# Landmark attention into a Fourier-mixed MLP: eight second halves of each weight matrix made on another engine, and the pseudo-inverse's product split off

## The chip, the core and the metric

The kernel runs on one core of a Trainium2 chip. The core has five engines that run side by side and signal each other by semaphores: TensorE (PE, matmuls; PEld is its loading of weights), VectorE (DVE), ScalarE (ACT), GpSimd (POOL) and SyncE (SP), which here issues the DMAs. Matmuls write to PSUM, eight banks of 128 partitions by 512 f32; all else lies in SBUF. The metric is device time in microseconds of one execution; the span that the profile shows runs from the first to the last instruction of it.

## The reference

There are two parts. The first is Nyström attention for 8 batches, 8 heads, 576 tokens of 64 channels, with 32 landmarks, each the mean of 18 tokens:

```python
A  = softmax(q    @ k_lm.T / 8)      # 576 x 32
Bm = softmax(q_lm @ k_lm.T / 8)      # 32 x 32
C  = softmax(q_lm @ k.T / 8)         # 32 x 576
Z  = Bm.T / (norm1(Bm) * norminf(Bm) + 1e-6)
for _ in range(6):
    Z = 2 * Z - Z @ Bm @ Z
x  = A @ Z @ C @ v
```

The second takes the result as rows of 512 (the heads side by side), applies a Fourier transform over tokens and one over channels, and keeps the real part; `u = x + mixed`; the rows of `u` are normalised to `un`; the output is `u + relu(un @ w1) @ w2`, with `w1` of 512 x 2048 and `w2` of 2048 x 512. The weights come as float64.

## The kernel before

**The large matmuls are done in f16, in two halves.** A number is scaled by a power of two, `hi` is its f16 rounding, and `lo` the f16 rounding of the difference; a product is then three f16 products (`mm3`). `split` (line 209) makes the halves: ScalarE writes `hi`, then VectorE writes `lo = src * scale - hi`.

**Weights (thread `weights`, line 233).** Each matrix lies in 16 pieces of 128 x 512. A piece arrives as 64-bit numbers, is decoded into f32 by three VectorE instructions and one of ScalarE (lines 250 and 287 to 289), and lies then in slot `f + 1` of its matrix. When all pieces of a matrix are decoded, their largest magnitude gives the scale (`scale`, line 260, with a transpose and a small product on TensorE in `pow2`). `halve` (line 268) then splits piece `f` into slot `f`, the two f16 halves side by side where a f32 piece lay before; the next piece's halves overwrite the slot that this piece's source was in. First come the 16 decodes of the first matrix; then, for each of the second matrix's 16 decodes, one `halve` of the first; then the second matrix's 16 `halve`s.

**Attention (threads `attention`, `tokens`, `landmarks`).** `tokens` (line 358) forms landmark sums, the scores A, their exponentials and the token side of the transform. `landmarks` (line 503), spawned by it, computes Bm (four heads to a group, two groups), its row-normalised form `nrm` beside the row sums spread over a diagonal, then for each group the product for C with maximum, exponential and sum (`Ces`, line 540), then the sum over columns `psn` with `ones_bd` (line 568), which gives the factor `ci`, then the transpose `BT` of the block matrix `Bbd`, then transposes of C, then C @ v. With E = I - c B B^T and R = c C v, the six steps of the iteration are carried out on R: `RE` holds E's 32 condensed columns beside R's 64, and each step multiplies both by E (line 621): one product of 96 columns for each group, then VectorE masks E into blocks and adds R, and ScalarE copies the condensed E. `Bbd` applied to the result gives W (line 636), its scale, its halves `Wx` and `Wt`, and their products with the transform (`WC`); `mix` forms `u`, and `norm` the statistics of its rows, `un`, and its two halves, which DMA transposes bring to `unT`. For batch 0 `norm` takes the statistics on ScalarE, for the others with BATCH_NORM_STATS2 on VectorE (line 754).

**MLP (thread `mlp`, line 803).** Rows go in 18 chunks of 256. A chunk has eight steps: a step of the first layer uses two pieces of `w1` (24 matmuls of 256 columns into a PSUM bank of `ps_h`, which has two; then ReLU and halves on ScalarE and VectorE), a step of the second (`second`, line 809) two pieces of `w2` (12 matmuls of 512 columns into `acc`). Each step waits until its pieces have been split (`split_w`). The first chunk keeps all eight hidden tiles until the second matrix is there, four of them in `mid` buffers, of which there are seven.

**What sets the order.** The threads are Python generators. A planner (`run`, line 871) keeps a clock `now` and prices for each instruction, and lets the first thread go whose time has come, by priority: `landmarks` before `attention`, `weights` and `mlp`. `till` makes a thread yield until the tiles named are expected to be there. TensorE executes the matmuls in exactly the order in which the planner let them be written; the order of the other engines' instructions is found by the framework's scheduler, with the order of writing as priority. Two waits of the planner hold batch 1 back: in `tokens` (line 414) and in `landmarks` (line 537) it goes on when four steps of the second layer have been written.

Of the kernel before, what the change touches and what calls it, by code (L numbers as in the profile page):

```python
# [10 lines left out]
F32 = mybir.dt.float32  # L11
F16 = mybir.dt.float16
# [113 lines left out]
class Kernel:  # L126
    def __init__(self, ctx, tc, NB, q, k, v, w1, w2, t1, t1t, t2, diag, mask, out):
# [71 lines left out]
    def tr(self, out, a, ident):  # L199
        self.there[out.name] = self.now  # L200
        self.now += 0.11
        self.nc.tensor.transpose(out, a, ident)  # L202
# [30 lines left out]
    def weights(self):  # L233
        nc = self.nc
        V, A = self.V, self.A
        whole = self.whole
        slots = [[t[:, i] for i in range(NF + 1)] for t in whole]
        am = [self.cp.tile([P, NF], F32, name=f"wmax{w}") for w in range(2)]
# [14 lines left out]
        def bound(i):  # L253

            w, f = pieces[i]
            A.activation(mags[i], slots[w][f + 1], AF.Abs, accum_out=am[w][:, f : f + 1])

        es = []

        def scale(w):  # L260
            a2 = self.small(1, "wm2")
            V.tensor_reduce(a2, am[w], AX.X, ALU.max)
            yield self.till(a2)
            e, r = yield from self.pow2(a2, 1, f"wp{w}")
            es.append(e)
            V.tensor_scalar(sc[:, w : w + 1], r[:, 0:1], (2.0**6, 2.0**14)[w], None, ALU.mult)

        def halve():
            w, f = pieces[sum(self.split_w)]
            self.split(hl[w][f][:, 0], hl[w][f][:, 1], slots[w][f + 1], sc[:, w : w + 1])  # L270
            self.split_w[w] = f + 1

        for i, (w, f) in enumerate(pieces):
            while len(mags) < min(2 * NF, i + 1 + PREP):
                j = len(mags)
                while len(self.wraw) < min(2 * NF, j + 1 + AHEAD):
                    self.raw()
                if self.raw_there[j] > self.now:
                    if j > i:
                        break  # L280
# [5 lines left out]
            x, dst = mags[i].bitcast(I32), slots[w][f + 1]  # L286
            V.tensor_scalar(x, x, 3, None, ALU.logical_shift_left)
            V.scalar_tensor_tensor(x, top, -0x80000000, x, ALU.bitwise_and, ALU.bitwise_or)
            V.scalar_tensor_tensor(dst.bitcast(I32), low, 29, x, ALU.logical_shift_right, ALU.bitwise_or)
            if i > 0:  # L290
                bound(i - 1)
            self.decoded = i + 1
            if self.decoded == 2 * NF:
                self.load(1)
            yield max(0.0, max(self.V.free, self.G.free) - self.now - WT)
            if i == NF:
                yield from scale(0)
            if es:
                halve()
                yield max(0.0, max(self.V.free, self.G.free) - self.now - WT)  # L300
# [3 lines left out]
        self.inv2 = sc[:, 2:3]  # L304
        while sum(self.split_w) < 2 * NF:
            halve()
            yield max(0.0, max(self.V.free, self.A.free) - self.now - WT)
# [50 lines left out]
    def tokens(self, b, st):  # L358
# [46 lines left out]
        for g in range(2):  # L405
# [95 lines left out]
        st["tokens"] = [*st["AT"], CS]  # L501

    def landmarks(self, b, st):
# [4 lines left out]
        m4g = lambda m: self.mask4.unsqueeze(1).unsqueeze(3).broadcast_to([P, 2, 4, m])  # L508
        wide = lambda src, m: src.unsqueeze(2).broadcast_to([P, 2, 4, m])
        Bd = sm.tile([P, 2, 32], F32, name="Bd")  # L510
        RE = sm.tile([P, 2, 96], F32, name="RE", bufs=3)
        Ces, crs = [], []
# [23 lines left out]

        while b == 1 and self.seconds < NF // 2 - HB:
            yield 0.5

        for g in range(2):  # L540
# [23 lines left out]
            crs.append(cr)  # L564
        yield self.till(nrm)

        psn = self.psum()
        mm(psn[:, 0:128], self.ones_bd.rearrange("p a b -> p (a b)"), nrm.rearrange("p g x m -> p (g x m)"))
        cm = self.small(4, "cm")
        V.tensor_reduce(cm, psn[:, 0:128].rearrange("p (x m) -> p x m", m=32), AX.X, ALU.max)  # L570
        ci = self.small(2, "ci")
        cmv = cm.rearrange("p (g x) -> p g x", x=2)
        V.tensor_tensor(ci, cmv[:, :, 0], cmv[:, :, 1], ALU.mult)
        V.tensor_scalar(ci, ci, 1e-6, None, ALU.add)
        V.reciprocal(ci, ci)
        nci = self.small(2, "nci")
        V.tensor_scalar(nci, ci, -1.0, None, ALU.mult)
        Bbd = sm.tile([P, 2, 4, 32], F32, name="Bbd", bufs=1)
        V.tensor_tensor(Bbd, wide(nrm[:, :, 0, :], 32), m4g(32), ALU.mult)
        yield self.till(Bbd, Ces[0])  # L580
        pst = self.psum()
        for g in range(2):
            tr(pst[:, 128 * g : 128 * g + 128], Bbd[:, g].rearrange("p a b -> p (a b)"), self.ident)
        BT = sm.tile([P, 2, P], F32, name="BT", bufs=1)
        A.copy(BT.rearrange("p g m -> p (g m)"), pst[:, 0:256])
        ETs = []
        for g in range(2):
# [8 lines left out]
            ETs.append(ET)  # L596
            if g == 0:
                yield self.till(BT, Ces[1])
                pse = self.psum()
                for i in range(2):  # L600
                    mm(pse[:, 128 * i : 128 * i + 128], BT[:, i], BT[:, i])
                E = sm.tile([P, 2, 4, 32], F32, name="E")
                for i in range(2):
                    V.scalar_tensor_tensor(
                        E[:, i].rearrange("p a b -> p (a b)"), pse[:, 128 * i : 128 * i + 128], nci[:, i : i + 1],
                        self.ident, ALU.mult, ALU.add,
                    )
                V.tensor_reduce(RE[:, :, 0:32], E.rearrange("p g a b -> p g b a"), AX.X, ALU.add)
        for g in range(2):
# [3 lines left out]
            for t in range(5):  # L613
                n = P if t < 4 else 64
                for i in range(4):
                    mm(ps[32 * i : 32 * i + 32, 0:64], ETs[g][:n, t, 32 * i : 32 * i + 32], vf[:n, t, 64 * i : 64 * i + 64], t == 0, t == 4)
            V.tensor_scalar(RE[:, g, 32:96], ps[:, 0:64], crs[g], ci[:, g : g + 1], ALU.mult, ALU.mult)
        yield self.till(E, RE)


        for it in range(6):
            c0 = 0 if it < 5 else 32
            ps = self.psum()
            for g in range(2):
                mm(ps[:, 96 * g + c0 : 96 * g + 96], E[:, g].rearrange("p a b -> p (a b)"), RE[:, g, c0:])
            pv = ps[:, 0:192].rearrange("p (g m) -> p g m", g=2)
            nRE = sm.tile([P, 2, 96], F32, name="RE", bufs=3)
            if it < 5:
                E = sm.tile([P, 2, 4, 32], F32, name="E")
                V.tensor_tensor(E, wide(pv[:, :, 0:32], 32), m4g(32), ALU.mult)  # L630
                A.copy(nRE[:, :, 0:32], pv[:, :, 0:32])
            V.tensor_tensor(nRE[:, :, 32:96], RE[:, :, 32:96], pv[:, :, 32:96], ALU.add)
            RE = nRE
            yield self.till(E, RE, more=NM)

        ps, pst = self.psum(), self.psum()
        for g in range(2):
            mm(ps[:, 64 * g : 64 * g + 64], Bbd[:, g].rearrange("p a b -> p (a b)"), RE[:, g, 32:])
# [110 lines left out]
    def norm(self, b, uts):  # L749
# [121 lines left out]
    def run(self):  # L871
# [3 lines left out]
        self.ulive, self.ufree, self.first_done, self.seconds, self.folded = 0, [], 0, 0, -1  # L875
        self.split_w, self.decoded = [0, 0], 0
        self.threads = []
# [83 lines left out]
```

## Time and profile before

| | |
|---|---|
| median of 3 runs | 1067.77 us (1065.95 to 1068.18) |
| the profiled execution | 1067.68 us, span 1065.9 us |
| TensorE, VectorE, ScalarE, GpSimd busy | 981.1, 614.0, 351.7, 126.6 us |
| TensorE's granted clock, mean | 0.960 |
| first matmul of the MLP | 104.70 us |
| first and last `lo` of the first matrix's halves (VectorE) | 92.69, 138.27 us |
| first and last `lo` of the second matrix's halves (VectorE) | 148.31, 187.63 us |
| first matmul of C, batch 1 | 166.81 us |

Times within the profile count from the span's start. A line of the time-ordered view gives start, duration, engine, line of the code (L197 is the helper `mm`, L202 `tr`, L121 the helper that emits for VectorE, ScalarE and GpSimd), operation, written tile `<-` read tiles, shapes, count, and in brackets the idle time before it with what ended it. Since almost all instructions go through helpers, tiles tell the groups apart: `w<-w,wsc` on VectorE is a `lo` of the weights, `h<-unT,w` the first layer, `acc<-w,h` the second, `at<-RE,E` the iteration, `at<-big,qbd` C. A matmul's duration includes its way through the array; how long one holds the engine is read from the start of the next. An f32 product is two MATMUL instructions in the profile.

### The profile page before, as it was taken

Reading aid. Unit: us, or ns where it says so; the run is one execution under the profiler, and the core shown is the slowest. Engines: PE = TensorE matmul, PEld = TensorE weight load, DVE = VectorE, ACT = ScalarE, POOL = GpSimd, SP = SyncE. Lnnn points to the kernel's source line nnn. Section 1 sums busy time; section 2 is a strip of 40 time slices with the busy share of each in tenths; the row PEclk is TensorE's granted clock in tenths of the full one; section 3 lists DMA queues with packets and bytes.
Section 4 is the critical chain, followed back from the end, with each engine's and each line's share of the span. In section 5 each row is a group of like instructions: output and inputs, shape, how many; then the busy total and the mean of one; then the engine's idle time right before and its main releaser. Section 6 shows DMA issues by size and latency. Waiting matters only on the chain.

```text
span 1065.9 us, 19548 instructions
## 1 busy us (share of the span) xinstructions
PE 981.1 (92%) x8008; PEld 681.0 (64%) x8008; DVE 614.0 (58%) x1655; ACT 351.7 (33%) x791; POOL 126.6 (12%) x137
## 2 busy tenths in 40 slices
PE   1553779999999999999999999999999999999998
PEld 0442645677776677766776777667766677766665
DVE  7889888768553476446746574567451654341111
ACT  4566755324221333124322332243312332111110
POOL 0101101021101030110302030104010030110000
PEclk8556989999999999999999999999999999999999
DMA  9824402221401022111502050114111010120000
GB/s 328 311 83 129 141 25 91 70 42 39 152 21 35 26 80 103 21 31 21 179 4 50 11 164 19 40 21 129 64 41 21 21 23 20 21 50 16 5 21 20
DMA packets 85994, 71.70 MB, mean 67 GB/s; under 512 B 56336, under 2 KB 74768, under 8 KB 85776
## 3 DMA queue, kind: packets, MB, share of 16 engines
q1 hardware_dynamic: 85904, 70.45, 22.1%
q8 instruction: 63, 1.03, 0.4%
q14 instruction: 27, 0.22, 0.1%
HBM read 48.02 MB, written 9.44 MB: 54 GB/s over the span
## 4 chain that ended last, share of the span: by engine, by line
PE 86%; DVE 8%; issue 2%; ACT 2%; DMA 1%; POOL 0%; SPq 0%; ACTq 0%; DVEq 0%
PE acc L197 34%; PE h L197 34%; PE at L197 16%; DVE w L121 2%; DVE row L121 2%; DVE mid L121 1%; PE at L202 1%; ACT row L121 1%; DVE lm L121 1%; DMA big<-q_dram 0%; ACT mid L121 0%; DVE asum L121 0%; DVE u L121 0%; DVE RE L121 0%; POOL row L121 0%
## 5 line engine op out<-in xcount | busy, mean ns | idle before, releaser
L197 PE MATMUL h<-unT,w 128*128 128x256 f16 x3456 | 413.5, 274 | 20.3 <-DMA unT<-row 11.5
L197 PEld LDWEIGHTS <-w 128*128 128x128 f16 x3456 | 336.2, 98 | 92.8 <-issue 19.5
L197 PE MATMUL acc<-w,h 128*128 128x512 f16 x1680 | 394.8, 379 | 0.0
L197 PEld LDWEIGHTS <-h 128*128 128x128 f16 x1680 | 161.9, 98 | 160.5 <-issue 3.4
L121 DVE SCALAR_TENSOR_TENSOR h<-h 128x512 f16<-128x512 f32 x140 | 96.5, 689 | 247.5 <-ACT h L121 247.0
L121 ACT ACTIVATE h<-h 128x512 f16<-128x512 f32 x140 | 83.4, 596 | 367.9 <-PE h L197 367.5
L121 POOL TENSOR_TENSOR r<-ve,mhalf 128x2 f32<-128x2 f32 (+1 forms) x20 | 13.7, 683 | 446.7 <-DVE ve L121 446.7
L121 POOL TENSOR_TENSOR row<-row 128x512 f16<-128x512 f32 (+1 forms) x44 | 47.3, 1089 | 44.0 <-ACT row L121 44.0
L197 PEld LDWEIGHTS <-mid 128*128 128x128 f16 x432 | 40.2, 103 | 17.7 <-issue 9.0
L197 PEld LDWEIGHTS <-big 128*128 128x128 f16 (+1 forms) x768 | 41.3, 106 | 13.6 <-issue 2.4
L121 POOL TENSOR_TENSOR mid<-mid,asum 128x512 f32<-128x512 f32 x14 | 15.1, 1080 | 272.2 <-issue 134.5
L121 DVE TENSOR_REDUCE lm<-big 128x32 f32<-128x576 f32 (+1 forms) x48 | 44.2, 945 | 3.3 <-DMA big<-k_dram 3.2
L121 DVE SCALAR_TENSOR_TENSOR row<-at,scw,row 128x262 f32<-128x262 f32 (+1 forms) x48 | 21.4, 486 | 41.4 <-ACT row L121 27.2
L121 ACT CAST row<-row 128x512 f16<-128x512 f32 (+1 forms) x44 | 23.2, 557 | 64.5 <-DVE row L121 63.9
L121 ACT ACTIVATE row<-w 128x512 f32<-128x512 f32 x54 | 33.8, 641 | 22.8 <-DVE w L121 12.4
L197 PE MATMUL at<-RE,E 128*128 128x96 f32 (+1 forms) x192 | 31.1, 288 | 9.0 <-DVE RE L121 9.0
L121 DVE SCALAR_TENSOR_TENSOR u<-at,scw,row 128x128 f32<-128x128 f32 (+3 forms) x120 | 38.9, 389 | 0.0
L121 POOL TENSOR_TENSOR mid<-mid 128x256 f32<-128x256 f32 (+1 forms) x32 | 31.5, 987 | 61.5 <-DVE mid L121 54.0
L197 PEld LDWEIGHTS at<-RE,E 128*128 128x128 f32 x192 | 28.6, 205 | 15.3 <-issue 6.2
L121 DVE TENSOR_TENSOR mid<-mid 128x256 f32<-128x256 f32 x48 | 34.5, 743 | 1.6 <-POOL mid L121 1.4
L197 PE MATMUL at<-mid,big 128*128 128x262 f16 (+1 forms) x288 | 34.3, 293 | 0.0
L121 DVE SCALAR_TENSOR_TENSOR u<-acc,wsc,u 128x512 f32<-128x512 f32 x36 | 26.7, 745 | 11.5 <-PE acc L197 11.3
(167 smaller groups left out, 955.6 us busy)
## 6 DMA issues: line engine op xcount, KB each, us to landing
w<-w_dram SPq DMA_DIRECT2D x22, 512.0 KB, 8.9
big<-v_dram SPq DMA_DIRECT2D x16, 640.0 KB, 9.2
big<-q_dram SPq DMA_DIRECT2D x16, 584.0 KB, 5.2
big<-k_dram SPq DMA_DIRECT2D x16, 576.0 KB, 4.2
out_dram<-u SPq DMA_DIRECT2D x36, 256.0 KB, 2.0
big<-w_dram SPq DMA_DIRECT2D x10, 512.0 KB, 8.2
unT<-row SPq DMA_TRANSPOSE x72, 2.4
t<-t_dram SPq DMA_DIRECT2D x1, 1048.0 KB, 9.2
```

The source lines that it names most:

```text
L121: return call(out, *args, **kw)
L197: self.nc.tensor.matmul(out, a, b, start=start, stop=stop, skip_group_check=True)
L202: self.nc.tensor.transpose(out, a, ident)
```

## The change

1. **Lower halves.** Pieces with odd `f` of both matrices no longer have their `lo` made by VectorE. TensorE multiplies the f32 source by an f32 identity times the scale, adds the f16 product of `hi` with minus the identity into the same PSUM tile (from `ps_h`), and ScalarE copies that tile to `lo`. The first matrix gets one more slot, so its source lies two slots ahead of its halves (`f + 2`) and not one; the second keeps one. In the first matrix an odd piece's TensorE part is written with the next piece's `halve`, in the second at once, behind a `till(hi)`.
2. **The iteration in a thread of its own.** `inverse`, spawned by `landmarks`, carries out the six steps on the condensed P (32 columns) and not on R (64): `EP` of 64 columns holds E and P. The first step multiplies 32 columns, the last 32, those between 64. A block product G = P^T Bbd follows, and `landmarks`, which keeps R apart, waits for G and applies it where it applied `Bbd` before.
3. **Order in `landmarks`.** The sum over columns `psn` and `ci` now come before the products of C.
4. **The second batch.** Both waits of batch 1 end after one step of the second layer, not four.
5. **Statistics.** `norm` uses ScalarE's passes for batch 1 as well as for batch 0.

```diff
-        self.whole = [self.cp.tile([P, NF + 1, 512], F32, name=f"w{w}") for w in range(2)]
+        self.whole = [self.cp.tile([P, NF + 2 - w, 512], F32, name=f"w{w}") for w in range(2)]
...
+        self.minus = self.cp.tile([P, P], F16, name="minus")
+        nc.vector.tensor_scalar(self.minus, self.ident, -1.0, None, ALU.mult)
...
             V.tensor_scalar(sc[:, w : w + 1], r[:, 0:1], (2.0**6, 2.0**14)[w], None, ALU.mult)
+            V.tensor_scalar(scaled[w], self.ident, sc[:, w : w + 1], None, ALU.mult)
...
         def halve():
-            w, f = pieces[sum(self.split_w)]
-            self.split(hl[w][f][:, 0], hl[w][f][:, 1], slots[w][f + 1], sc[:, w : w + 1])
-            self.split_w[w] = f + 1
+            w = 0 if self.begun[0] < NF else 1
+            f = self.begun[w]
+            hi, lo, src = hl[w][f][:, 0], hl[w][f][:, 1], slots[w][f + 2 - w]
+            if f % 2 == 0:
+                self.split(hi, lo, src, sc[:, w : w + 1])
+            else:
+                A.activation(hi, src, AF.Copy, scale=sc[:, w : w + 1])
+            self.begun[w] += 1
+            left.append((w, f, hi, lo, src))
+            while left and (left[0][1] % 2 == 0 or len(left) > 1 - left[0][0] or self.begun[0] == NF):
+                w, f, hi, lo, src = left.pop(0)
+                if f % 2:
+                    yield self.till(hi)
+                    ps = self.ps_h.tile([P, 512], F32, name="h")
+                    self.mm(ps, scaled[w], src, True, False)
+                    self.mm(ps, self.minus, hi, False, True)
+                    A.copy(lo, ps)
+                self.split_w[w] = f + 1
...
-        while b == 1 and self.seconds < NF // 2 - HB:
+        while b == 1 and self.seconds < 1:
             yield 0.5
...
+    def inverse(self, st, nrm, nci):
...
+        for it in range(6):
+            yield self.till(E, EP, banks=1, more=NM)
+            c0, c1 = (0 if it < 5 else 32), (64 if it > 0 else 32)
+            ps = self.psum()
+            for g in range(2):
+                mm(ps[:, 64 * g + c0 : 64 * g + c1], flat(E, g), EP[:, g, c0:c1])
...
+        yield self.till(Pbd, banks=1)
+        ps = self.psum()
+        for g in range(2):
+            mm(ps[:, 128 * g : 128 * g + 128], flat(Pbd, g), flat(Bbd, g))
+        G = sm.tile([P, 2, 4, 32], F32, name="G", bufs=1)
+        A.copy(G.rearrange("p g a b -> p (g a b)"), ps[:, 0:256])
+        st["G"] = G
...
+        self.spawn(self.inverse(st, nrm, nci))
+
+        while b == 1 and self.seconds < 1:
             yield 0.5
...
-            V.tensor_scalar(RE[:, g, 32:96], ps[:, 0:64], crs[g], ci[:, g : g + 1], ALU.mult, ALU.mult)
-        yield self.till(E, RE)
-
-
-        for it in range(6):
-            c0 = 0 if it < 5 else 32
-            ps = self.psum()
-            for g in range(2):
-                mm(ps[:, 96 * g + c0 : 96 * g + 96], E[:, g].rearrange("p a b -> p (a b)"), RE[:, g, c0:])
...
+            V.tensor_scalar(R[:, g], ps[:, 0:64], crs[g], ci[:, g : g + 1], ALU.mult, ALU.mult)
+
+        while "G" not in st:
+            yield 0.3
+        Gt = st["G"]
+        yield self.till(Gt, R, banks=2)
...
-                mm(pst[64 * o : 64 * o + 64, 64 * g : 64 * g + 64].rearrange("p (r m) -> p r m", r=2), RE[:, g, 32:], Bbd[:, g, o::2])
+                mm(pst[64 * o : 64 * o + 64, 64 * g : 64 * g + 64].rearrange("p (r m) -> p r m", r=2), R[:, g], Gt[:, g, o::2])
...
-        if b == 0:
+        if b < 2:
```

More of the change, by code (lines that the diff above doesn't have):

```diff
@@ L236, in weights @@
         whole = self.whole
-        slots = [[t[:, i] for i in range(NF + 1)] for t in whole]
+        slots = [[t[:, i] for i in range(NF + 2 - w)] for w, t in enumerate(whole)]
         am = [self.cp.tile([P, NF], F32, name=f"wmax{w}") for w in range(2)]
@@ L255, in bound @@
             w, f = pieces[i]
-            A.activation(mags[i], slots[w][f + 1], AF.Abs, accum_out=am[w][:, f : f + 1])
+            A.activation(mags[i], slots[w][f + 2 - w], AF.Abs, accum_out=am[w][:, f : f + 1])
         es = []
@@ L266, in scale @@
             V.tensor_scalar(sc[:, w : w + 1], r[:, 0:1], (2.0**6, 2.0**14)[w], None, ALU.mult)
+            V.tensor_scalar(scaled[w], self.ident, sc[:, w : w + 1], None, ALU.mult)
+            self.begun[w] = 0
+        scaled = [self.cp.tile([P, P], F32, name=f"wid{w}") for w in range(2)]
+        left = []
         def halve():
-            w, f = pieces[sum(self.split_w)]
-            self.split(hl[w][f][:, 0], hl[w][f][:, 1], slots[w][f + 1], sc[:, w : w + 1])
-            self.split_w[w] = f + 1
+            w = 0 if self.begun[0] < NF else 1
[16 more added lines that the diff above has]
+                self.split_w[w] = f + 1
         for i, (w, f) in enumerate(pieces):
@@ L298, in weights @@
             if es:
-                halve()
+                yield from halve()
                 yield max(0.0, max(self.V.free, self.G.free) - self.now - WT)
@@ L304, in weights @@
         self.inv2 = sc[:, 2:3]
-        while sum(self.split_w) < 2 * NF:
-            halve()
+        while sum(self.begun) < 2 * NF:
+            yield from halve()
             yield max(0.0, max(self.V.free, self.A.free) - self.now - WT)
@@ L501, in tokens @@
         st["tokens"] = [*st["AT"], CS]
+    def inverse(self, st, nrm, nci):
+        mm, tr, sm, V, A = self.mm, self.tr, self.sm, self.V, self.A
+        m4 = self.mask4.unsqueeze(1).unsqueeze(3).broadcast_to([P, 2, 4, 32])
+        wide = lambda t: t.unsqueeze(2).broadcast_to([P, 2, 4, 32])
+        flat = lambda t, g: t[:, g].rearrange("p a b -> p (a b)")
+        Bbd = sm.tile([P, 2, 4, 32], F32, name="Bbd", bufs=1)
+        V.tensor_tensor(Bbd, wide(nrm[:, :, 0, :]), m4, ALU.mult)
+        yield self.till(Bbd, banks=1)
+        ps = self.psum()
+        for g in range(2):
+            tr(ps[:, 128 * g : 128 * g + 128], flat(Bbd, g), self.ident)
+        BT = sm.tile([P, 2, P], F32, name="BT", bufs=1)
+        A.copy(BT.rearrange("p g m -> p (g m)"), ps[:, 0:256])
+        yield self.till(BT, nci, banks=1)
+        ps = self.psum()
+        for g in range(2):
+            mm(ps[:, 128 * g : 128 * g + 128], BT[:, g], BT[:, g])
+        E = sm.tile([P, 2, 4, 32], F32, name="E")
+        for g in range(2):
+            V.scalar_tensor_tensor(flat(E, g), ps[:, 128 * g : 128 * g + 128], nci[:, g : g + 1], self.ident, ALU.mult, ALU.add)
+        EP = sm.tile([P, 2, 64], F32, name="EP", bufs=3)
+        V.tensor_reduce(EP[:, :, 0:32], E.rearrange("p g a b -> p g b a"), AX.X, ALU.add)
+        for it in range(6):
+            yield self.till(E, EP, banks=1, more=NM)
+            c0, c1 = (0 if it < 5 else 32), (64 if it > 0 else 32)
+            ps = self.psum()
+            for g in range(2):
+                mm(ps[:, 64 * g + c0 : 64 * g + c1], flat(E, g), EP[:, g, c0:c1])
+            pv = ps[:, 0:128].rearrange("p (g m) -> p g m", g=2)
+            nEP = sm.tile([P, 2, 64], F32, name="EP", bufs=3)
+            if it < 5:
+                nE = sm.tile([P, 2, 4, 32], F32, name="E")
+                V.tensor_tensor(nE, wide(pv[:, :, 0:32]), m4, ALU.mult)
+                A.copy(nEP[:, :, 0:32], pv[:, :, 0:32])
+            if it == 0:
+                V.tensor_tensor(nEP[:, :, 32:64], EP[:, :, 0:32], self.diag32.unsqueeze(1).broadcast_to([P, 2, 32]), ALU.add)
+            else:
+                V.tensor_tensor(nEP[:, :, 32:64], EP[:, :, 32:64], pv[:, :, 32:64], ALU.add)
+            E, EP = nE, nEP
+        yield self.till(EP, banks=1)
+        Pbd = sm.tile([P, 2, 4, 32], F32, name="E")
+        V.tensor_tensor(Pbd, wide(EP[:, :, 32:64]), m4, ALU.mult)
+        yield self.till(Pbd, banks=1)
+        ps = self.psum()
+        for g in range(2):
+            mm(ps[:, 128 * g : 128 * g + 128], flat(Pbd, g), flat(Bbd, g))
+        G = sm.tile([P, 2, 4, 32], F32, name="G", bufs=1)
+        A.copy(G.rearrange("p g a b -> p (g a b)"), ps[:, 0:256])
+        st["G"] = G
@@ L535, in landmarks @@
         )
-        while b == 1 and self.seconds < NF // 2 - HB:
+        yield self.till(nrm)
+        psn = self.psum()
+        mm(psn[:, 0:128], self.ones_bd.rearrange("p a b -> p (a b)"), nrm.rearrange("p g x m -> p (g x m)"))
+        cm = self.small(4, "cm")
+        V.tensor_reduce(cm, psn[:, 0:128].rearrange("p (x m) -> p x m", m=32), AX.X, ALU.max)
+        ci = self.small(2, "ci")
+        cmv = cm.rearrange("p (g x) -> p g x", x=2)
+        V.tensor_tensor(ci, cmv[:, :, 0], cmv[:, :, 1], ALU.mult)
+        V.tensor_scalar(ci, ci, 1e-6, None, ALU.add)
+        V.reciprocal(ci, ci)
+        nci = self.small(2, "nci")
+        V.tensor_scalar(nci, ci, -1.0, None, ALU.mult)
+        self.spawn(self.inverse(st, nrm, nci))
+        while b == 1 and self.seconds < 1:
             yield 0.5
@@ L564, in landmarks @@
             crs.append(cr)
[L565 to L581, printed above, removed]
-        for g in range(2):
-            tr(pst[:, 128 * g : 128 * g + 128], Bbd[:, g].rearrange("p a b -> p (a b)"), self.ident)
-        BT = sm.tile([P, 2, P], F32, name="BT", bufs=1)
-        A.copy(BT.rearrange("p g m -> p (g m)"), pst[:, 0:256])
+        yield self.till(Ces[0])
         ETs = []
@@ L596, in landmarks @@
             ETs.append(ET)
[L597 to L608, printed above, removed]
         for g in range(2):
```

20 lines of the change are left out of this document (4 added, 16 removed).

## The prediction

> **What bounds the kernel now.** I read the page first (busy shares and the forty slices), then cut the span into stages, then read TensorE and VectorE in order of time inside the stages that are not full. The page:
>
> ```profile
> PE 981.1 (92%) x8008; PEld 681.0 (64%) x8008; DVE 614.0 (58%) x1655; ACT 351.7 (33%) x791; POOL 126.6 (12%) x137
> PE   1553779999999999999999999999999999999998
> DVE  7889888768553476446746574567451654341111
> PEclk8556989999999999999999999999999999999999
> ```
>
> A slice is 26.6 us. TensorE reaches 9 tenths in the seventh slice (from 160 us) and keeps them; before that it has 1 to 7, and VectorE 7 to 9. The stage table has, for each stretch, its length, then busy time and count of PE, PEld, DVE, ACT, POOL, and the granted clock:
>
> ```profile
> 27.70:46.60 18.90, 11.75 (x165) 9.96 (x166) 15.87 (x49) 10.34 (x24) 0.00 (x0) 0.59 1.07 371
> 46.60:66.80 20.20, 12.09 (x67) 9.50 (x65) 17.65 (x41) 11.56 (x29) 4.47 (x5) 0.58 0.10 41
> 66.80:104.70 37.90, 14.97 (x91) 10.26 (x91) 34.45 (x90) 25.48 (x63) 4.23 (x3) 0.64 0.46 139
> 104.70:144.50 39.80, 30.79 (x235) 23.50 (x235) 36.12 (x70) 29.13 (x61) 3.75 (x3) 0.90 0.40 120
> 148.30:166.80 18.50, 16.17 (x54) 6.03 (x53) 13.67 (x35) 10.20 (x17) 0.00 (x0) 0.76 0.11 33
> 166.80:200.00 33.20, 29.89 (x332) 20.26 (x332) 28.34 (x77) 15.84 (x39) 6.94 (x8) 1.00 0.21 64
> 200.00:225.00 25.00, 23.94 (x192) 17.39 (x190) 18.97 (x58) 9.22 (x23) 2.96 (x3) 1.00 0.24 73
> 225.00:1060.00 835.00, 833.43 (x6840) 580.17 (x6838) 423.99 (x1170) 227.22 (x508) 102.23 (x107) 1.00 0.17 47
> ```
>
> Three regimes follow. From 225 us TensorE is busy 833.43 of 835 at full clock: a microsecond of matmul added there is a microsecond of time, and one taken from VectorE or ScalarE is nothing. Until 144.5 us VectorE sets the pace (36.12 of 39.80 in the last stretch), with TensorE waiting. Between 148.3 and 225 both matter: TensorE is idle for 2.33 + 3.31 + 1.06 = 6.7 us, and a clock of 0.76 over 16.17 us costs 3.9 more; 10.6 us are lost in all. So the end is the moment at which the second matrix's halves can start, plus all matmul work from there, plus what is lost on the way to 225.
>
> That moment:
>
> ```profile
> 138.27 0.76 DVE L121 SCALAR_TENSOR_TENSOR w<-w,wsc 128x512 f16<-128x512 f32 x1
> 144.47 0.27 PE L202 MATMUL at<-ident,wm 128*1 128x128 f32 x1
> 147.56 0.72 ACT L121 ACTIVATE w<-w,wsc 128x512 f16<-128x512 f32 x1 [6.38 <-DVE wsc L121]
> 148.31 0.75 DVE L121 SCALAR_TENSOR_TENSOR w<-w,wsc 128x512 f16<-128x512 f32 x1
> 140.00:144.50 4.50, 4.50 (x29) 3.36 (x26) 3.87 (x8) 0.88 (x3) 0.00 (x0) 0.62 0.00 0
> ```
>
> VectorE finishes the first matrix's last lower half at 138.27; TensorE then runs the last hidden-layer matmuls, busy throughout at a clock of 0.62; only behind them, in order, comes the transpose for the second matrix's scale (144.47), and the first split of it starts at 147.56.
>
> **The change part by part: lower halves.** Sixteen of the 32 subtractions leave VectorE, eight from each matrix. One occupies the engine for as long as it takes to the start of the next instruction:
>
> ```profile
> 130.81 0.75 DVE L121 SCALAR_TENSOR_TENSOR w<-w,wsc 128x512 f16<-128x512 f32 x1
> 131.47 0.69 DVE L121 SCALAR_TENSOR_TENSOR h<-h 128x512 f16<-128x512 f32 x1
> ```
>
> 0.66 us. In the first matrix that frees 8 x 0.66 = 5.3 us of the engine that sets the pace. The scaled identity costs it something between nothing and 0.66 (the same kind of operation with four times the columns); I take 0.2. For each odd piece TensorE gets an f32 product with 512 columns and an f16 product with 512, and ScalarE a copy out of PSUM. No f32 product of that width is in the trace; the nearest are these, each read to the start of the row behind it:
>
> ```profile
> 227.00 0.86 PE L197 MATMUL at<-mid,big 128*64 128x262 f16 x12
> 227.69 0.82 PE L197 MATMUL at<-Wx,row 128*64 128x256 f16 x6
> 309.74 1.52 PE L197 MATMUL at<-mid,big 128*128 128x262 f16 x12
> 311.10 1.47 PE L197 MATMUL at<-Wx,mid 128*128 128x256 f16 x12
> 240.52 2.14 PE L197 MATMUL at<-big,qbd 128*64 128x288 f32 x16
> 242.59 0.82 PE L197 MATMUL acc<-w,h 128*128 128x512 f16 x3
> ```
>
> With all 128 columns of weights an f16 matmul of 262 takes (311.10 - 309.74) / 12 = 0.113 us; with 64, (227.69 - 227.00) / 12 = 0.058, half: two that write different halves of PSUM's partitions run together. The f32 row has weights of 64 columns as well, and 2 instructions to each of the 8 products in the code: 2.07 / 16 = 0.129 us. Taken at its face that is 2 x 0.129 x 512 / 288 = 0.46 us for a new product; if those too ran in pairs it is twice that, 0.92. The f16 pair decides me for 0.92. With 0.113 x 512 / 262 = 0.22 for the f16 product a half costs 1.14 us of TensorE, at least 0.68. The Trainium skill, "FP8 and Floating Point Precision", section TensorE Precision Notes, has a true FP32 product take four passes; four passes of 512 at the 0.22 us of an f16 product would be 0.88 us, as an estimate, and the trace's pairs agree with it. Read at one pass to an instruction, the sum below would come out at 1060.3.
>
> In the first matrix the eight halves fall into gaps (TensorE idles 9.0 us between 104.7 and 144.5 and more before), all but the last, which stands ahead of the scale's transpose: +1.1 on the way to 148.3. If the gaps didn't take them, 8 x 1.14 = 9.1 would be lost there. In the second matrix they fall where TensorE is nearly full: 8 x 1.14 = **+9.1** (at least 5.4).
>
> ```profile
> L121 ACT COPY mid<-at 128x512 f32<-128x512 f32 x16 | 9.2, 576 | 2.0 <-PE at L202 1.6
> ACT w L121 <- DVE w L121: 13.5, 14, 1.9
> ```
>
> ScalarE's sixteen copies at 0.58 us lie beside VectorE (ScalarE is busy 29.13 of 39.80); without that cover they cost 8 x 0.58 = 4.6 per matrix. Here is also the new wait. Today an upper half waits for the lower half before it, whose source it overwrites (13.5 us in 14 waits). The extra slot undoes that in the first matrix only. In the second, after an odd piece, the next upper half waits until TensorE has read the source; queued behind it on ScalarE stand the copies and the exponentials of the second batch, and TensorE, in order, waits for the copy before the matmuls that use it.
>
> **The clock and the last hidden-layer matmuls.** The clock of 0.62 over 4.5 busy us costs 1.7. With halves between them TensorE rests less; I take the 1.7 back, at worst nothing. The second matrix's first split then starts 5.3 - 0.2 - 1.1 + 1.7 = **5.7 us** earlier, near 142.
>
> **The thread of its own.** In the first batch the iteration no longer stands behind exponentials, transposes and the product with v; it can fill VectorE's idle time while those run. That idle time is 18.90 - 15.87 + 20.20 - 17.65 = 5.6 us from 27.7 to 66.8. I take half, **-2.8**, bounds 0 and -5.6. VectorE's own work in it hardly changes: one masking more, six narrower additions. TensorE's side for each batch:
>
> ```profile
> 256.82 0.58 PE L197 MATMUL at<-RE,E 128*128 128x96 f32 x4
> 257.24 2.10 PE L197 MATMUL acc<-w,h 128*128 128x512 f16 x9
> 286.54 0.56 PE L197 MATMUL at<-RE,E 128*128 128x64 f32 x4
> 286.94 2.13 PE L197 MATMUL h<-unT,w 128*128 128x256 f16 x18
> 250.64 0.61 PE L197 MATMUL at<-BT 128*128 128x128 f32 x4
> 251.09 0.71 PE L202 MATMUL at<-ident,mid 128*128 128x128 f32 x5
> ```
>
> An iteration with 96 columns takes 0.42 us and one with 64 takes 0.40, so narrowing saves at most 6 x 0.02 a batch; I take nothing. The product G is two f32 products of 128 columns, like BT's: 0.45 us. In batches 1 to 7 TensorE is full: 7 x 0.45 = **+3.2**, bounds 2.3 and 3.2. In batch 0 it idles and nothing is paid. The copy of G and the wait for it lie behind the matmuls of other threads; without them a batch would wait one copy, 0.58.
>
> The sum over columns is also moved, ahead of the first batch's C:
>
> ```profile
> 12.30 4.09 PE L197 MATMUL at<-big,qbd 128*64 128x288 f32 x16
> 29.37 0.20 DVE L121 TENSOR_TENSOR nrm<-diag,rs 128x64 f32<-128x64 f32 x1
> 29.72 0.77 PE L197 MATMUL at<-nrm,ones_bd 128*128 128x128 f32 x2 [1.66 <-DVE nrm L121]
> L121 DVE TENSOR_REDUCE cmx<-at 128x1 f32<-128x288 f32 x32 | 14.4, 451 | 2.6 <-PE at L197 2.5
> ```
>
> C's 16 matmuls run at 12.30 now; in TensorE's order they would stand behind a product that could not start before 29.4, with their four reductions (4 x 0.45 = 1.8 us) then in VectorE's full time. VectorE can decode weights instead meanwhile, so I take zero, with +1.8 in a rival.
>
> **The second batch let go** after one second-layer step rather than four: its scores and C, now at 166.8, can start beside the second matrix's halves; the third batch's six loads follow on SP's queue as much earlier, with DMA shares of 0.11 to 0.24 there. The gaps of 148.3 to 225 are what they can fill. I take a third of the idle time as left (2.2 of 6.7) and 1.0 of the clock's 3.9: 10.6 - 3.2 = **-7.4**, bounds 0 and -10.6. Four `mid` tiles are still held by the first chunk's hidden layer then, so later tiles of this batch may have to wait for steps two to four; with that it would start no earlier than now.
>
> **The second batch's statistics on ScalarE** take five BATCH_NORM_STATS2 off VectorE and put ten passes on ScalarE, near 217 to 235 us, under a full TensorE: nothing either way.
>
> **The sum**: -5.7 - 2.8 + 9.1 + 3.2 - 7.4 = -3.6. The profiled execution took 1067.68 (span 1065.9, 1.8 around it), against a median of 1067.77, so the two can be used alike. Forecast: **1064.0 us**.
>
> **The rivals.** *Slower: TensorE's waits take the place of VectorE's.* In the second matrix an odd piece now goes ScalarE, TensorE, ScalarE, and TensorE is in order: if for each it stands for an upper half (0.72) or a copy (0.58), eight pieces lose 5 to 6 us and batch 1's help is used up. With nothing of the 10.6 recovered: -5.7 - 2.8 + 9.1 + 3.2 = +3.8, 1071.5. It is slower than before as soon as fewer than 3.8 us of the 10.6 come back. For it: two thirds of the loss is idle time, and 14 waits of this very kind. Against it: each second-layer step has four matmuls before it needs the odd lower half.
>
> *More than forecast.* The second batch closes the whole loss and the threads all of VectorE's idle time: -5.7 - 5.6 + 9.1 + 3.2 - 10.6 = -9.6, 1058.1. For it: VectorE has 4.8 idle us of 18.5 where today the second batch stands still. Against it: some waits in 166.8 to 225 are the second batch's own chain.
>
> *The thread brings nothing.* C behind the sum over columns: +1.8 in place of -2.8: -5.7 + 1.8 + 9.1 + 3.2 - 7.4 = +1.0, 1068.7. For it: the row at 29.37. Against it: the decode that can fill the time.
>
> **How the numbers follow.** About 0.2% (2.1 us) is what a measurement here can tell from no change: below 1065.6 is faster, above 1069.9 slower. Chances: the forecast (1061 to 1065.6) 0.30, more than that 0.20, the thread without gain or the like (1065.6 to 1069.9) 0.23, slower 0.27. So faster 0.50, same 0.23, slower 0.27. The likeliest case's own range is 1061 to 1065.6; cases of both signs are near, so the range goes to 1056 and 1072.5, past both outer rivals by 1 to 2 us for the prices of f32.
>
> **What would show it.** The first split of the second matrix near 142; TensorE's f32 product of 512 columns at about 0.92 us to the next start; PE idle time between that split and 225 down to 2 to 3 us with the clock at 0.9 or more; C of batch 1 before 160; G's four matmuls at 0.45 in every batch. I am wrong if the split does not move (TensorE, not VectorE, held the first matrix), if the product takes 0.46, or if the idle time stays at 6 us with waits on `w` from ScalarE.

## The result: slower by 30 us

The changed kernel takes 1096.99 us (median of 4 runs, 1096.54 to 1098.68) against 1066.86 for the kernel before beside it (1065.36 to 1068.18): ratio 1.0286, interval 1.0266 to 1.0305. The forecast was 1064.0 (its own sum gives 1064.1), with a range up to 1072.5.

The page of the changed kernel, in the rows that answer to those of before:

```profile
span 1095.3 us, 19764 instructions
...
PE 998.6 (91%) x8088; PEld 689.9 (63%) x8088; DVE 608.1 (56%) x1646; ACT 369.0 (34%) x835; POOL 125.1 (11%) x137
...
PE   0654888899999999999999999999999999999998
...
PEclk9756999999999999999999999999999999999999
```

TensorE has 17.5 us more busy time and the span 29.4 us more length. TensorE's nine tenths begin two slices later than before (the ninth slice, from 219 us, against the seventh, from 160). The stage table (length, then busy time and count of PE, PEld, DVE, ACT, POOL, then TensorE's granted clock):

```profile
148.30:166.80 18.50, 15.26 (x107) 8.88 (x106) 14.99 (x61) 11.13 (x26) 0.00 (x0) 0.91 0.28 96
166.80:200.00 33.20, 27.52 (x260) 16.47 (x258) 24.60 (x63) 14.75 (x32) 6.97 (x8) 0.95 0.19 59
200.00:225.00 25.00, 22.42 (x150) 13.70 (x149) 15.01 (x42) 15.07 (x38) 2.96 (x3) 1.00 0.10 20
225.00:1060.00 835.00, 823.77 (x6784) 575.61 (x6783) 426.81 (x1175) 232.15 (x524) 101.68 (x107) 1.00 0.17 48
```

Two things are to be seen. From 148.3 to 225 TensorE idles 3.24 + 5.68 + 2.58 = 11.5 us, where it idled 6.7; the clock did come up from 0.76 to 0.91 in the first of these windows, but fell from 1.00 to 0.95 in the second. And from 225 on, where the kernel before lost 1.6 us in 835, 11.2 are lost. Its waits there (engine, tile and line, the releaser, then total, times and longest):

```profile
PE at L204 <- ACT mid L121: 8.5, 6, 1.6
PE acc L199 <- DVE u L121: 1.7, 1, 1.7
PE at L199 <- DVE nrm L121: 0.7, 2, 0.3
```

L204 is the transpose helper, and the time-ordered view shows one of the six:

```profile
251.35 0.39 PE L199 MATMUL at<-nrm,ones_bd 128*128 128x128 f32 x2
251.66 2.16 PE L199 MATMUL at<-big,qbd 128*64 128x288 f32 x16
255.14 0.27 PE L204 MATMUL at<-ident,amax 128*4 128x128 f32 x1 [1.31 <-ACT mid L121]
```

The column sums, C's eight products (16 instructions) and then, right behind them in TensorE's order, the transpose of the token maxima (`pow2` of `tokens`). C fills four tiles of `ps_at`, which has four banks; the transpose needs the first of them back, and waits until ScalarE has read it for the exponential. In the kernel before other work stood between:

```profile
240.52 2.14 PE L197 MATMUL at<-big,qbd 128*64 128x288 f32 x16
242.59 0.82 PE L197 MATMUL acc<-w,h 128*128 128x512 f16 x3
243.25 1.47 PE L197 MATMUL h<-unT,w 128*128 128x256 f16 x12
244.56 0.41 PE L197 MATMUL at<-nrm,ones_bd 128*128 128x128 f32 x2
244.80 0.27 PE L202 MATMUL at<-ident,amax 128*4 128x128 f32 x1
```

There C was written without a yield, the thread then yielded for `nrm`, and 244.56 - 242.59 = 1.97 us of MLP matmuls came before the next tile of `ps_at`. With the sums moved ahead, it is C that ends the step, and the planner puts the transpose next.

### The profile page after: what moved, and what is told of

Read it like the earlier page. It is cut to its first block, busy times and chain, and to the rows that moved or that the text cites. A ratio compares the mean times of both kernels' runs of the same rounds, so it can differ in the third digit from the quotient of the medians.

```text
span 1095.3 us, 19764 instructions
## 1 busy us (share of the span) xinstructions
PE 998.6 (91%) x8088; PEld 689.9 (63%) x8088; DVE 608.1 (56%) x1646; ACT 369.0 (34%) x835; POOL 125.1 (11%) x137
## 4 chain that ended last, share of the span: by engine, by line
PE 81%; DVE 8%; issue 5%; ACT 3%; DMA 2%; POOL 1%; SPq 0%; ACTq 0%; POOLq 0%
PE h L199 33%; PE acc L199 33%; PE at L199 14%; DVE row L121 1%; DVE mid L121 1%; DVE cmx L121 1%; PE at L204 1%; ACT mid L121 1%; DMA big<-q_dram 1%; DVE w L121 1%; ACT big L121 1%; ACT w L121 1%; ACT h L121 1%; DMA big<-v_dram 1%; POOL mid L121 0%
## 5 line engine op out<-in xcount | busy, mean ns | idle before, releaser
L199 PEld LDWEIGHTS at<-EP,E 128*128 128x128 f32 x192 | 29.1, 207 | 13.4 <-issue 6.4
L199 PE MATMUL at<-EP,E 128*128 128x64 f32 (+1 forms) x192 | 29.5, 280 | 6.9 <-DVE EP L121 6.7
```

What stands on the lines that cost most here:

```text
L199: self.nc.tensor.matmul(out, a, b, start=start, stop=stop, skip_group_check=True)
```

## The experiments

Ratios are to the kernel before on the same chip, with their intervals; a percent is 10.7 us. None of these kernels leaves out work of the reference; one does a product twice.

**The parts one by one.** Each takes a part of the diff alone; the last is the changed kernel with the block of the column sums moved behind C again.

```diff
# halves_alone: hunks of part 1 only     # thread_alone: parts 2 and 3 only
# letgo_alone: part 4 only, in both waits
-        while b == 1 and self.seconds < NF // 2 - HB:
+        while b == 1 and self.seconds < 1:
# c_first: the changed kernel, in landmarks
-        yield self.till(nrm)
-        psn = self.psum()
...
-        self.spawn(self.inverse(st, nrm, nci))
         while b == 1 and self.seconds < 1:
             yield 0.5
         for g in range(2):
...
             crs.append(cr)
+        yield self.till(nrm)
+        psn = self.psum()
...
+        self.spawn(self.inverse(st, nrm, nci))
```

> Only the lower halves of odd pieces on TensorE, all else as before. If the cost of the change is the sum of its parts (theory P), this one takes the eight halves of the second matrix, 8 x 1.08 = 8.6 us, plus a few us for TensorE's waits there: 10 to 14 us slower than before, and the first split of the second matrix not earlier than 146. If the loss comes from all parts meeting in one written order (theory O), it is within 5 us of before.

Measured 1074.27 us, 1.0075 (1.0056 to 1.0095): 8.0 us, between the two expectations.

> Only the iteration's thread with the column sums ahead of C; the second batch held back as before, statistics as before. Theory P: G's 0.45 us in seven batches (3.2) and the wait of the transpose of amax for a bank that C holds (8.5 us in 6 batches of the changed kernel): 9 to 14 us slower than before, with that wait in the list of TensorE's waits. Theory O: 2 to 4 us slower, G alone.

Measured 1086.12, 1.0184 (1.0165 to 1.0204): 19.6 us, more than either expectation.

> Only the second batch let go after one step of the second layer. Theory P: it fills idle time between 148 and 225, 0 to 5 us faster than before. Theory O: its matmuls push the second matrix's steps back in TensorE's order, 0 to 5 us slower.

Measured 1068.51, 1.0025 (1.0012 to 1.0039): 2.7 us slower, as theory O has it.

> The changed kernel with C's products written ahead of the column sums again, the thread kept. Theory P: the transposes of amax no longer wait for C's banks, 7 to 10 us faster than the changed kernel (near 1087 to 1090), and that wait is gone from the list. Theory O: the wait moves to another instruction and the time stays within 3 us of the changed kernel's 1097.

Measured 1086.30, 1.0186 (1.0166 to 1.0205): 0.0100 or 10.7 us come back, and TensorE is busy 833.16 us of the 835 from 225 to 1060, as before, in place of 823.77. So none of these parts gains anything, and a move that I priced at nothing is the dearest.

**The column sums.** The move alone, and the thread without it:

```diff
# c_late_alone: the kernel before, psn to nci moved ahead of C, nothing else
# thread_c_first: parts 2 and 3, with C written first as in c_first
```

> The kernel before with one thing moved: C's products, maxima and exponentials are written behind the column sums, as in the changed kernel; no thread, no lower half on TensorE. Theory P (a price for each part): the transpose of amax stands behind C in TensorE's order and waits for a PSUM bank, 1.2 to 1.6 us in six or seven batches, so 8 to 11 us slower than before. Theory T (the wait belongs to the thread, whose own products take the banks): within 3 us of before.

Measured 1087.49, 1.0198 (1.0182 to 1.0213): 21.1 us, twice what theory P has and far from theory T. Not all of it is the full stage: the MLP's first matmul comes at 114.32 us, where it was 104.70.

> The iteration's thread alone, with C's products ahead of the column sums as before. Theory P: the 20 us of the thread alone were some 10 of banks and 3.2 of G, and the rest a later first batch; without the wait for banks it is 8 to 11 us slower than before. Theory T: nothing but the order in TensorE was at fault, and with C first it is 2 to 4 us slower (G alone).

Measured 1071.95, 1.0055 (1.0039 to 1.0072): 5.9 us, between the two expectations. Then the transpose alone was moved, by planned time, in the kernel with only the sums ahead and in the changed kernel:

```diff
-        yield self.till(am, more=AM)
+        yield self.till(am, more=AM + 5.0)
         e, r = yield from self.pow2(am, 4, "ab")
```

> The kernel before with the column sums ahead of C, and the transpose of the token maxima written five units of planned time later, which puts 2.6 us of MLP matmuls between C's last product and it in batches 2 to 7. Theory O (the loss of about 10 us in the full stage is this transpose waiting for C's banks): TensorE's idle time from 225 to 1060 us falls from 12.2 to below 3 us, the wait on ScalarE's exponential of C at the transposes from 20.7 us to below 5, and the time from 1.020 of before to 1.007 to 1.012 (the part lost in the first batch, 8 us, stays). Theory P (the transpose is only where a shortage of banks shows; the next tile asked for will wait as long): idle stays above 9 us at another line, and the ratio at 1.016 or more.

Measured 1072.13, 1.0050 (1.0032 to 1.0068), less than theory O's 1.007 to 1.012.

> The changed kernel whole, with nothing altered but that the transpose of the token maxima is written five units of planned time later (2.6 us of MLP matmuls between C's last product and it in batches 2 to 7). Theory O: the idle time of 11.2 us from 225 to 1060 falls below 3, and the time by 8 to 10 us, to 1.019 to 1.021 of before, where C ahead of the column sums brought it too (1.0186). Theory P: within 2 us of the changed kernel, 1.027 or more.

Measured 1087.66, 1.0197 (1.0181 to 1.0212). The window from 225 to 1060 in each kernel (length, TensorE's busy time and count, clock, DMA share, GB/s); of the kernel with the sums ahead:

```profile
225.00:1060.00 835.00, 822.81 (x6767) 1.00 0.17 48
```

the same with the transpose later:

```profile
225.00:1060.00 835.00, 834.33 (x6862) 1.00 0.17 48
```

and the changed kernel with the transpose later:

```profile
225.00:1060.00 835.00, 832.98 (x6852) 1.00 0.17 48
```

Idle time falls from 12.2 to 0.7 and from 11.2 to 2.0, and the waits for `mid` at the transpose are gone, with the sums still ahead of C. So the loss in the full stage is this one wait, and in the changed kernel a shift of a 0.27 us transpose by 2.6 us of other work takes away 9.5 of the 10.7 us. With the sums alone ahead of C, 5.4 us (1.0050) stay that are not this wait; there the MLP still begins at 112.64, not 104.70. Theory P, a shortage of banks that would show up elsewhere, falls. The Trainium skill, "Perfetto Trace Analysis", section Optimization Strategy, says that the same gap repeated on an engine that should be full can mean that there is no PSUM for the next tile. The trace agrees (six gaps of up to 1.6 us), but here the order was at fault and the number of banks was enough. One difference stays open in the main: alone, the shift brought 0.0148 or 15.8 us where the idle time of the window fell by 11.5; the MLP's start, 114.32 to 112.64, can be 1.7 us of the rest.

**G written twice.** The thread with C first, and one line more:

```diff
+        for g in range(2):
+            mm(ps[:, 128 * g : 128 * g + 128], flat(Pbd, g), flat(Bbd, g))
```

> The thread with C ahead of the column sums (1.0055 of before), with the four matmuls of G written twice into the same bank, so that each batch does 0.45 us more on TensorE and nothing else changes. If work in TensorE's full stage costs its own length (the forecast's term of 3.2 us for G): 7 x 0.45 = 3.2 us more, 1.0075 to 1.0095. If such small groups hide in gaps that are there anyway, and the thread's cost is all in the first 110 us: 1.0045 to 1.0065, as without.

Measured 1074.62, 1.0073 (1.0058 to 1.0088), 0.0018 or 1.9 us more than with one G. Its row, and the next, in the full stage:

```profile
290.53 1.06 PE L197 MATMUL at<-Bbd,E 128*128 128x128 f32 x8
291.42 2.75 PE L197 MATMUL acc<-w,h 128*128 128x512 f16 x12
```

Eight hold TensorE for 0.89 us, so four for 0.45, as the forecast had it. The time lies between the two expectations, and the intervals don't tell whether 1.9 or the full 3.2 are paid.

**The halves of one matrix, and the start of the second.** The first kernel keeps part 1 for the first matrix alone; the second is the kernel before with the ninth first-layer step of the MLP held until two pieces of the second matrix are split, so that the scale's transpose doesn't stand behind it:

```diff
# halves_first_alone
-                if f % 2:
+                if f % 2 and w == 0:
# pair_back, in mlp
+            while ch == 1 and self.split_w[1] < 2:
+                yield 0.5
```

> The kernel before with the odd lower halves of the first matrix alone on TensorE; the second matrix as before. Theory P: the 8.6 us of the eight halves alone on TensorE were those of the second matrix, 8 x 1.08, so this one is within 2 us of before, although VectorE ends the first matrix some 3 to 5 us earlier, because the second matrix's scale stands behind TensorE's hidden-layer matmuls and halves. Theory V (VectorE set that end): 4 to 6 us faster than before.

Measured 1066.44, 0.9995 (0.9984 to 1.0007).

> The kernel before with the ninth step of the first layer held back until the second matrix's first two pieces are split. If TensorE's order, not VectorE, sets the start of the second matrix (theory P), its scale's transpose comes 2 to 3 us earlier and the time is 0 to 3 us below before. If VectorE sets it (theory V), the transposes move by less than 1 us and the time is within 1 us of before or above it.

Measured 1066.53, 0.9998 (0.9989 to 1.0008). What becomes of VectorE's freed time shows in the kernel with the first matrix's halves only (start, duration, operation, idle time before it):

```profile
135.72 0.15 DVE L121 TENSOR_REDUCE wm<-wmax 128x1 f32<-128x16 f32 x1
```

```profile
134.02 1.02 PE L199 MATMUL h<-w,wid 128*128 128x512 f32 x2
134.88 0.38 PE L199 MATMUL h<-w,minus 128*128 128x512 f16 x1
135.69 2.78 PE L199 MATMUL h<-unT,w 128*128 128x256 f16 x24 [0.42 <-DVE h L121]
138.30 1.02 PE L199 MATMUL h<-w,wid 128*128 128x512 f32 x2
139.16 0.38 PE L199 MATMUL h<-w,minus 128*128 128x512 f16 x1
139.88 3.44 PE L199 MATMUL h<-unT,w 128*128 128x256 f16 x30 [0.34 <-DVE h L121]
143.15 0.27 PE L204 MATMUL at<-ident,wm 128*1 128x128 f32 x1
```

The maximum of the second matrix is reduced at 135.72, where it was 141.5 before: VectorE is 5.8 us ahead, as forecast. But its transpose stands behind two more hidden-layer steps and two more halves in TensorE's order, and starts at 143.15, 1.3 us earlier than before. And where the start did come earlier, by 147.56 - 144.99 = 2.6 us with the step held back, nothing came of it either: the first matmul of the second layer then stood behind the step that had been held, at 150.23 in place of 148.3.

**The second batch beside the halves.** The kernel without the thread has parts 1, 4 and 5; the next leaves part 5 out as well; and part 5 alone:

```diff
# no_thread: parts 1, 4, 5     # halves_letgo: parts 1, 4     # stats_alone: part 5
-        if b == 0:
+        if b < 2:
```

> The change without the thread and with C where it was: the second halves on TensorE in both matrices, the second batch let go, the statistics of the second layer on ScalarE. If the parts add (8.0 us for the halves and 2.8 us for the second batch, alone): 10.8 us, 1.008 to 1.012 of before. If letting the second batch go only costs time where it meets the halves' tiles in the hidden-layer banks, the two together cost more than their sum: 1.014 or above. If the halves make room that the second batch uses: 1.007 or less.

Measured 1085.04, 1.0170 (1.0154 to 1.0185).

> The second halves on TensorE and the second batch let go, without the statistics of the second layer on ScalarE and without the thread: the kernel without the thread (1.0170) less one part. Theory S (the 7 us by which halves, second batch and statistics together exceed the sum of halves and second batch alone come from the statistics, which put ScalarE behind in the second matrix): 1.010 to 1.012. Theory I (the second batch's attention and the second matrix's halves hold each other up while both are written between 150 and 225 us): 1.0155 or more, with TensorE idle 13 us or more from 150 to 225 and a granted clock below 1.00 there.

Measured 1083.72, 1.0171 (1.0157 to 1.0186), as theory I has it; from 150 to 225 TensorE idles 12.8 us (13 or more were expected) at a clock of 0.91.

> The kernel before with only the statistics of the second batch's second layer on ScalarE. The forecast priced them at nothing: 0.9985 to 1.0015. Theory S: a loss of its own, 1.003 to 1.007, between 150 and 225 us.

Measured 1067.08, 1.0005 (0.9996 to 1.0014). The statistics cost nothing; the halves and the second batch, 0.0075 and 0.0025 alone, are 0.0171 together: 0.0071 or 7.6 us exist only where both are there. The upper halves of the second matrix (16, with first and last start) and the first chunk's second-layer matmuls show where. Of the halves alone:

```profile
L121 ACT ACTIVATE w<-w,wsc x16: 721/721/743, 147.2 to 191.3; 128x512 f16<-128x512 f32 x16
L199 PE MATMUL acc<-w,mid x48: 376/379/389, 150.1 to 165.2; 128*128 128x512 f16 x48
```

of the second batch let go alone:

```profile
L121 ACT ACTIVATE w<-w,wsc x16: 709/722/722, 147.2 to 186.7; 128x512 f16<-128x512 f32 x16
L197 PE MATMUL acc<-w,mid x48: 376/379/631, 148.0 to 174.0; 128*128 128x512 f16 x48
```

and of both:

```profile
L121 ACT ACTIVATE w<-w,wsc x16: 710/722/740, 144.9 to 213.2; 128x512 f16<-128x512 f32 x16
L199 PE MATMUL acc<-w,mid x48: 378/379/634, 147.9 to 190.2; 128*128 128x512 f16 x48
```

Together they stretch the splitting to 68 us, where it takes 44 and 40 with either alone and took 36.7 before (147.6 to 184.3). The window from 185 to 200 of the kernel with both (length, TensorE's busy time and count, clock, DMA share, GB/s) shows the price:

```profile
185.00:200.00 15.00, 10.26 (x65) 0.77 0.00 1
```

With no second-layer pieces to go on with, TensorE idles 4.7 of 15 us and falls to a clock of 0.77, in a stretch in which the kernel before was busy 13.90 at 1.00. Inside that window, two upper halves that follow each other and what TensorE does between them:

```profile
185.09 0.72 ACT L121 ACTIVATE w<-w,wsc 128x512 f16<-128x512 f32 x1 [0.35 <-DVE w L121]
194.19 2.90 PE L199 MATMUL at<-t,Wt 128*64 128x262 f16 x24 [3.58 <-ACT Wt L121]
197.02 2.07 PE L199 MATMUL h<-w,wid 128*128 128x512 f32 x2
199.19 0.72 ACT L121 ACTIVATE w<-w,wsc 128x512 f16<-128x512 f32 x1 [0.83 <-PE h L199]
```

For 14.1 us no upper half starts: TensorE waits 3.58 us for the second batch's `Wt`, does that batch's 24 products, and only then comes to the f32 product of the odd piece, which releases the next upper half. So each odd piece of the second matrix goes ScalarE, TensorE, ScalarE, and TensorE's order there now holds the second batch's products with their own waits. How much of the 7.6 us each of these waits costs was not taken apart.

**The parts that cost TensorE nothing, together.** The kernel before with the first matrix's halves, the step held back and the later transpose:

> The kernel before with the three edits that took idle time from TensorE without adding work to its full stage: the second halves of the first matrix alone on TensorE, the ninth first-layer step behind the second matrix's first two pieces, and the transpose of the token maxima five units of planned time later. If the two leads of the first two (3.1 and 1.7 us of MLP work ahead at 1000 us) and the idle time left in the full stage (1.6 us) add: 0.995 to 0.998. If, as with each of the first two alone, the lead goes into the last batch's tail: 0.9985 to 1.0005.

Measured 1065.78, 0.9994 (0.9984 to 1.0004): no difference. Nothing found here beats the kernel before.

## Why the prediction was wrong

The account, from the runs, each line one part more than the line above:

| kernel | ratio | us more |
|---|---|---|
| halves on TensorE | 1.0075 | 8.0 |
| and the second batch let go | 1.0171 | 10.2 |
| and the statistics | 1.0170 | 0 |
| and the thread, C first | 1.0186 | 1.7 |
| and the column sums ahead of C: the changed kernel | 1.0286 | 10.7 |

The shares hang on the order of the lines: alone, the second batch costs 2.7 us, the thread with C first 5.9 and the column sums 21.1.

- **"VectorE can decode weights instead meanwhile, so I take zero", for the column sums ahead of C: the step that failed most.** I had looked at that move in the first batch only, where it is visible, and priced VectorE's work there. It is made in all eight batches, and in six of them (batches 2 to 7) the place of C in TensorE's order decides whether a transpose waits for a bank; in batch 1 that transpose stands ahead of C. 10.7 us, of which 9.5 are that wait. The row that would have told it was in the trace before: the 1.97 us of MLP work between C and the next tile of `ps_at`.
- **The second batch let go, -7.4: wrong in sign.** +2.7 alone (0.0025), +10.2 beside the halves. The clock came back in the first window (0.76 to 0.91) and fell in the second (1.00 to 0.95), and C of the second batch began at 159.05, not 166.81; but I counted the gaps as room and not what is pushed aside. The products of the second batch stand in the same order as the second layer's, bring waits of their own, and delay the pieces on which the MLP depends. The idle time, to fall to 2 or 3 us, rose to 11.5.
- **The earlier start of the second matrix, -5.7: the mechanism fell.** VectorE does end earlier by what I worked out (5.8 us against 5.3 in the run with the first matrix's halves alone). That it was VectorE that set the start was the mistake, one of the three ways that I had named in which I would be wrong: the row at 144.47, which I had quoted, stood behind hidden-layer matmuls that run longer with the halves between them. In the changed kernel:

```profile
143.25 1.02 PE L199 MATMUL h<-w,wid 128*128 128x512 f32 x2
144.11 0.38 PE L199 MATMUL h<-w,minus 128*128 128x512 f16 x1
144.82 3.44 PE L199 MATMUL h<-unT,w 128*128 128x256 f16 x30 [0.33 <-DVE h L121]
148.10 0.27 PE L204 MATMUL at<-ident,wm 128*1 128x128 f32 x1
...
151.56 0.72 ACT L121 ACTIVATE w<-w,wsc 128x512 f16<-128x512 f32 x1 [3.32 <-DVE wsc L121]
```

  The first split is at 151.56, 4.0 us later than before, where I had 142; 2.8 us of that go with the column sums, since with C first it is at 148.74. And the run with the step held back shows that 2.6 us of an earlier start are worth nothing by themselves, so the step from start to end of the sum failed too.
- **The halves of the second matrix, +9.1: right in the price of a half, and near the total partly by luck.** A product to the next start takes 0.86 us, by 121.14 and 122.00 of the run with the halves alone:

```profile
121.14 1.02 PE L199 MATMUL h<-w,wid 128*128 128x512 f32 x2
122.00 0.38 PE L199 MATMUL h<-w,minus 128*128 128x512 f16 x1
...
152.69 1.02 PE L199 MATMUL h<-w,wid 128*128 128x512 f32 x2
153.55 0.38 PE L199 MATMUL h<-w,minus 128*128 128x512 f16 x1
153.77 1.03 PE L199 MATMUL acc<-w,mid 128*128 128x512 f16 x4
```

  With 0.22 for the f16 product (153.55 to 153.77) a half is 1.08 and eight are 8.6, against 0.92 + 0.22 = 1.14 and 9.1; the kernel with the halves alone lost 8.0 (6.0 to 10.1). But there TensorE's idle time from 148.3 to 225 rose from 6.7 to 9.8, against which the clock of the first window came back from 0.76 to 1.00, 3.9 us by the prediction's own reckoning; that the two nearly cancel was not forecast. The choice of 0.92 over 0.46, from the paired f16 rows, held. In the first matrix they cost nothing (0.9995). The Trainium skill's four passes ("FP8 and Floating Point Precision", TensorE Precision Notes) gave 0.88 as an estimate; the trace agrees.
- **G, +3.2: its length right (0.45), its price not settled** (1.9, with an interval that takes in 3.2). **The thread in the first batch, -2.8: the lead came and was worth nothing.** With C first the thread costs 0.0055 or 5.9 us; less 3.2 for G, 2.7 are lost where 2.8 were to be gained. The rows of that kernel:

```profile
64.09 0.68 PE L197 MATMUL at<-Bbd,E 128*128 128x128 f32 x4 [1.58 <-DVE E L121]
65.24 0.43 PE L197 MATMUL at<-R,G 128*128 128x64 f32 x2 [0.46 <-ACT G L121]
...
101.76 0.37 PE L197 MATMUL h<-unT,w 128*128 128x256 f16 x1 [12.05 <-DMA unT<-row]
...
144.73 0.58 PE L197 MATMUL acc<-w,mid 128*128 128x512 f16 x1 [2.27 <-ACT w L121]
```

  Before, the product with the block matrix started at 66.82, the MLP at 104.70 and its second layer at 148.33, so in this trace the three come 1.6, 2.9 and 3.6 us earlier. But from the second layer's start to 225 TensorE idles 10.0 us here (busy 70.27 of 80.27) and 6.7 before (70.00 of 76.67), and the lead is gone. It is the same step that failed for the second matrix: an earlier start is no earlier end. In the changed kernel not even the lead is there:

```profile
68.20 0.69 PE L199 MATMUL at<-R,G 128*128 128x64 f32 x2 [0.46 <-ACT G L121]
...
106.99 0.40 PE L199 MATMUL h<-unT,w 128*128 128x256 f16 x1 [11.66 <-DMA unT<-row]
```

  With C first these two are at 65.31 and 103.74, so the column sums ahead of C push the first batch back as well.
- **The statistics, nothing: right** (1.0005).
- **The slower rival** named the mechanism that the pair of halves and second batch shows (TensorE in order, waiting where VectorE waited), and was too small: it stopped at "nothing of the 10.6 recovered", though the stage could, and did, become worse than before. For an edit that reorders TensorE's work I let the bounds end at no gain, and the range with them.

## What to carry to other kernels

Where one engine's order is fixed by a planner, a moved block is priced at each place where it is executed, and by its neighbours: read which instruction will now stand next behind it, and whose buffers it has just filled. Idle time of the engine that is soon full need not be room for another thread's chain, when the work that ends the stage needs the same engine in order. And before counting on time that is freed on one engine, find the instruction that the next stage starts with, and see in the order what stands in front of it on its own engine.

## What the runs showed of the hardware

An f32 product with all 128 columns of weights takes nearly twice the time per instruction and column of one with 64: 0.43 us an instruction for 512 columns against 0.129 for 288, which would be 0.23 for 512; that fits the pairing that the f16 rows had shown. And a transpose of 0.27 us cost TensorE up to 1.6 us of waiting, six times and 8.5 us in all in a stretch of 835, while ScalarE, which it waits for, is busy 232.15 us of the 835.
